# Row E on SyncE's queue, one feature fold for two blocks, and batch 1's folds across spread over steps 24 to 29 on two engines

## The chip, the core and the metric

The kernel runs on one core of a Trainium2 chip. A core has five engines that this document speaks of: PE (TensorE, matrix products, with its weight loads listed apart as PEld), DVE (VectorE), ACT (ScalarE), POOL (GpSimd) and SP (SyncE, which only issues DMAs here). Each engine works through its own list of instructions in order and waits on semaphores for the others. ACT can issue DMAs too; such an issue, and whatever it waits for, stands in ACT's list between its computing instructions. The metric is device time in microseconds (us) of one execution.

## The reference

```python
X = np.fft.fft(x, axis=1); X = np.fft.fft(X, axis=2)     # x: (8, 3008, 256)
t = X.real.astype(np.float32).reshape(24064, 256)
gate = 1.0 / (1.0 + np.exp(-(t @ w_gate)))                # w_gate, w_val: (256, 1536)
out = (gate * (t @ w_val)) @ w_out                        # w_out: (1536, 256)
```

Everything is float32.

## The kernel before, in words

**Tiling.** A batch has S = 3008 rows. A row s, its mirror S-s and the two rows half a batch away are loaded side by side as the four parts `x4[:, 0..3]` of one tile (128 partitions x 4 parts x 6 row groups q x 256 features). Sums and differences of the parts ("folds") shrink the transform over rows, and sums and differences of features d and 256-d shrink the one over features. `fold_ops` lists the folds of a batch: `point` and `first` add the mirrored rows (L405, L409), `across` adds and subtracts parts 0 and 2 (L418), `feat` makes feature sums and differences of one block (L412 to L415). There are two blocks, for even and odd frequencies. The products with cosine and sine tables (`half`, sums into the banks `ev` and `od`) give PK (cosine of the feature sums) and QK (sine of the feature differences), written by `places` (L510, L513) after ACT has copied the bank `ev` (L505). The middle feature, number 128, has its own row: `e_sums` multiplies it with the tables into the bank `pe`, `even`, `rest` and `last` put it together in the tile `er`, and it goes out to the DRAM tensor `ed` (L572) and comes back spread over all partitions as `ek` (`e_rows`, L599).

**Steps.** Then come 288 tokens-by-features steps `i`, twelve to a group of columns (chunk). A step multiplies PK with G1 (`front_a`), ACT copies the result (`part`, L626, tile `ae`), PE adds QK times G2 into the same bank (`front_b`), so `front_b` must wait for `part`. ACT and DVE then gate it (`gate_a`, `gate_b`: L640, L641, L653, L654, L657), POOL forms sums of blocks (`H_SUMS`, L663, tile `sf`), and five steps later `back` multiplies them with output weights (`po`). Order inside a step on DVE: gate_a's L641, gate_b's L653 and L657, copies and sums of a finished chunk (`later`, L747), then the work that `at(i, ...)` put at step i. On ACT: L640, L626, the next step's `seed` (L611, twice), L654.

**The start.** Batch 0 is folded by DVE in three calls of `half_rows`, two row groups each; after each one PE multiplies what is ready: the cosine sums of block 0, row E (`e_`), the cosine sums of block 1. When all three are done come the copies and placements, ACT's first half of the weight job 2 (`weight_parts(2)`: L296, L297), ACT's DMA of row E, ACT's copy of it to `e0` (L837, into the tile `wqk`), the sine sums, ACT's jobs 3 and 5 with the two `ev` copies for QK between and behind them, ACT's DMA of `ek`, and step 0. Steps 0 to 4 take row E by two extra products with `e0`; from step 5 on, `seed` takes it from `ek`. Weight jobs are 512 KB loads by SP in the order 0, 1, then (behind batch 0's rows and tables) 2, 3, 5, 6, 8, 9, 4, 7, each with a pass over ACT (L296, L297), DVE (L306, L307, L309) and POOL (L311), then a product on PE (`ps`) and two ACT copies (L331, L332), and small DMAs of `ge` on SP (L334).

**DMA semaphores.** DMAs from SP and ACT take eight semaphores (DMAHW0 to 7) in turn in program order. An instruction that issues one waits first for the last DMA on its semaphore. In the program's list of waits the DMA of row E waits for DMAHW7, last used by weight job 8, and ACT's `ek` waits for DMAHW2 (job 7) besides row E.

**Batch 1's folds.** Their 24 operations are put at steps given by hand in `slots`: POOL's points and firsts at steps 20 to 24, six `across` on DVE, two each at steps 27, 28 and 29, POOL's feature folds and row sums from 31 on. Batch 1's PK and QK are computed at step 64. Rows E of batches 1 to 7 are made together: sums and the first `places` (in `even`) at step 40, an ACT copy (`rest`) at 41, the second `places` (`last`) and the DMA to `ed` at 42.

Of the kernel before, what the change touches and what calls it, by code (L numbers as in the profile page):

```python
# [12 lines left out]
ALU = mybir.AluOpType  # L13
# [40 lines left out]
NQ = 6  # L54
# [27 lines left out]
def kernel(  # L82
# [10 lines left out]
    nc = tc.nc  # L93
    B, _, _, _, D = xf.shape
    F = moe_w_gate.shape[1]
    P = 128
# [4 lines left out]
    NO = (M // 2) // 2  # L101
# [296 lines left out]
    def fold_ops(b, nq):  # L398
        x4 = X.pop(b)
        if not b:  # L400
            x4 = x4[0:NP]
        ops = []

        def point(e, i, j, q):
            e.tensor_tensor(x4[:, i, q, 1:D], x4[:, i, q, 1:D], x4[:, j, q, D - 1 : 0 : -1],  # L405
                            op=ALU.add)

        def first(e, i, j, q):
            e.tensor_tensor(x4[:, i, q, 0], x4[:, i, q, 0], x4[:, j, q, 0], op=ALU.add)  # L409

        def feat(e, v, r, q):
            e.memset(r[:, q, 0:1], 0.0)  # L412
            e.tensor_tensor(r[:, q, 1:HD], v[:, q, 1:HD], v[:, q, D - 1 : HD : -1],  # L413
                            op=ALU.subtract)
            e.tensor_tensor(v[:, q, 1:HD], v[:, q, 1:HD], v[:, q, D - 1 : HD : -1], op=ALU.add)  # L415

        def across(e, blk, q):
            e.tensor_tensor(x4[:, 1 - blk, q], x4[:, 0, q], x4[:, 2, q],  # L418
                            op=(ALU.add, ALU.subtract)[blk])

        parts = [(x4[:, 1], x4[:, 3]), (x4[:, 0], x4[:, 2])]
        qs = [slice(q, q + nq) for q in range(0, NQ, nq)]
        pool = nc.gpsimd
        if b:

            for i in (0, 2):
                ops += [lambda i=i, q=q: point(pool, i, i + 1, q) for q in qs]
                ops.append(lambda i=i: first(pool, i, i + 1, slice(0, NQ)))
            for blk in range(2):
                ops += [lambda blk=blk, q=q: across(nc.vector if b == 1 else pool, blk, q) for q in qs]  # L430
            ops += [lambda q=q: feat(pool, *parts[1], q) for q in qs]
            for i, op in enumerate((ALU.add, ALU.subtract)):
                for ds in (slice(0, HD), slice(HD, D)):
                    ops.append(lambda i=i, op=op, ds=ds: pool.tensor_tensor(
                        x4[:, 3, i * N3 : (i + 1) * N3, ds], x4[:, 1, 0:N3, ds],
                        x4[:, 1, N3:, ds], op=op))
            parts[0] = x4[:, 3], x4[:, 1]
            slots = x4.rearrange("p i q d -> p (i q) d")

            def turn(q, minus):  # L440

                y = [slots[:, q : q + 16 : 15], slots[:, q + N3 : q + N3 + 10 : 9]]
                if minus:
                    y.reverse()
                nc.vector.scalar_tensor_tensor(
                    out=y[0][:, :, HD:D], in0=y[1][:, :, 0:HD], scalar=(ST[3], ST[4])[minus][:, q : q + 1],
                    in1=y[0][:, :, 0:HD], op0=ALU.mult, op1=ALU.add)
            TURN[b] = [lambda q=q, minus=minus: turn(q, minus) for q in range(N3) for minus in range(2)]
            ops += [lambda q=q: feat(pool, *parts[0], q) for q in qs]
        else:  # L450

            def half_rows(q):
                even, odd = slice(0, 4, 2), slice(1, 4, 2)
                point(nc.vector, even, odd, q)
                first(nc.vector, even, odd, q)
                for blk in range(2):
                    across(nc.vector, blk, q)
                    feat(nc.vector, *parts[blk], q)
            ops += [lambda q=q: half_rows(q) for q in qs]
        for blk, (v, r) in enumerate(parts):  # L460
            if b and blk:
                W[b, blk] = v[:, :, HD:D], r[:, :, HD:D]
                continue
            W[b, blk] = v[:, :, 0:HD], r[:, :, 0:HD], v[:, :, HD : HD + 1]
        return ops
# [40 lines left out]
            return lambda: places(d, blk, sn, a, od)  # L506
        return sums, then, both

    def places(d, blk, sn, ev, od):
        nc.vector.tensor_tensor(d[:, blk : blk + 2 * ev.shape[1] - 1 : 2], ev, od, op=ALU.add)  # L510
        lo, hi = (od, ev) if sn else (ev, od)
        top = M - blk
        nc.vector.tensor_tensor(d[:, top : top - 2 * NO + 1 : -2], lo[:, 0:NO], hi[:, 0:NO],  # L513
                                op=ALU.subtract)

    def whole(b, blk, what):
        _, then, both = seq_group(b, blk, what, (2, 3) if what else (0, 1))
# [8 lines left out]
    def seq_group(b, blk, what, other=None):  # L526
        return half(b, lambda q: W[b, blk][what][:, q, :], PQE[b][what], blk, what == 1, other)
# [14 lines left out]
    def e_sums(m=B - 1):  # L542


        ps = bank("pe", NB - 1)
        at_ = lambda blk, par: slice((2 * blk + par) * TB, (2 * blk + par) * TB + m)

        def sums(*qs):
            for q in qs:
                for blk in range(2):  # L550
                    c0, n = ((0, NE), (NE, NO))[blk]
                    w = x8[:, :, 1 + 2 * blk, q] if m > 1 else W[0, blk][2][:, q]
                    mm(ps[at_(blk, q % 2), 0:n], w, ST[0][0:NP, 0, q, c0 : c0 + n], q < 2, q >= NQ - 2)

        def even():
            er = op.tile([P, NK + 1], F32, name="er", tag="os")[0:m]
            if m == 1:
                E0.append(er)
            nc.vector.memset(er[:, NK:], 0.0)
            a = evp.tile([P, 2 * NJ], F32, name="a", tag="a")[0:m, 0:NE]  # L560
            e1 = evp.tile([P, 2 * NJ], F32, name="a", tag="a")[0:m, 0:NE]
            nc.scalar.copy(a, ps[at_(0, 1), 0:NE])
            nc.scalar.copy(e1[:, 0:NO], ps[at_(1, 0), 0:NO])

            places(er, 0, True, a, ps[at_(0, 0), 0:NE])

            def rest():
                nc.scalar.copy(a[:, 0:NO], ps[at_(1, 1), 0:NO])

            def last():  # L570
                places(er, 1, False, e1[:, 0:NO], a[:, 0:NO])
                (nc.sync if m > 1 else nc.scalar).dma_start(out=ed[1:] if m > 1 else ed[0:1], in_=er)  # L572
            return rest, last
        return sums, even

    def e_joint():
# [17 lines left out]
    def e_rows(i):  # L594

        b, c, _ = groups[i // 3]
        k0, n = chunks[c]
        EK[i // NFT] = ekp.tile([P, CH], F32, name="ek", tag="ek")[:, 0:n]
        (nc.sync if i else nc.scalar).dma_start(out=EK[i // NFT], in_=ed[b : b + 1, k0 : k0 + n].to_broadcast([P, n]))  # L599

    PF, AP, Z = {}, {}, {}
    N1 = 5
# [222 lines left out]
    for i, f in enumerate(fold_ops(0, 2)):  # L825
        q = 2 * i, 2 * i + 1
        f()
        cos[0][0](*q)
        e_(*q)
        cos[1][0](*q)  # L830
    cos[0][1]()()
    cos[1][1]()()
    rest, last_ = e_even()
    rest()
    weight_parts(2)
    last_()
    nc.scalar.copy(e0[0:1], E0[0][:, 0:CH])  # L837
    sin = [seq_group(0, blk, 1, (2 * blk, 2 * blk + 1)) for blk in range(2)]
    for q in range(0, NQ, N3):
        for sums, _, _ in sin:  # L840
            sums(*range(q, q + N3))
# [13 lines left out]
    def at(i, *fs):  # L855
        side.setdefault(i, []).extend(fs)
# [29 lines left out]
    at(3 * i0 + 5, lambda: later_e[0]())  # L886
    at(3 * i0 + 6, lambda: later_e[1]())
    at(3 * i0 + 6, table_again)
    at(4 * i0 - 3, lambda: [at(i, f) for i, f in zip((50, 46, 48, 49, 51, 52), table_odd())])
    for i in range(i0, count, i0):  # L890
        at(i - (8 if i == i0 else 11), lambda i=i: e_rows(i))

    for b in range(B - 1):
        s0 = b * per
        g0 = s0 + 3 * i0 + 4 if b else 5 * i0 + 4


        slots = [i for i in range(s0 - 2 * i0 if b > 1 else s0 if b else 2 * i0, g0 - 2)
                 if i % i0 < (4 if b > 1 else 6)]

        def folds(slots, b=b):
            ops = fold_ops(b + 1, 2)
            for i, f in enumerate(ops):
                at(slots[i * len(slots) // len(ops)], f)
            for i, f in enumerate(TURN.pop(b + 1)):
                at(58 + i if b == 0 else slots[-1] - 1 + i * 4 // 6, f)
        if b == 0:

            slots = [20, 20, 21, 21, 22, 23, 24, 24, 27, 27, 28, 28, 29, 29, 31, 33, 35, 37, 39, 41, 44, 51, 54, 56]
            assert len(slots) == 24  # L910
        at(slots[0] - 1, lambda slots=slots, folds=folds: folds(slots))
        at(g0 - 2, lambda b=b: seq_start(b + 1))
        for blk in (1, 0):
            at(g0, *[lambda b=b, blk=blk, what=what: whole(b + 1, blk, what)() for what in range(2)])
        if b < B - 2:
            at(g0 + 1, lambda b=b: load_x(b + 2))
            for i, f in zip(calm(s0 if b else 3 * i0), mirror_x(b + 2)):
                at(i, f)
# [83 lines left out]
```

## Time and profile before

| | us |
|---|---|
| median of 3 runs (1931.51 to 1933.19) | 1932.86 |
| profiled execution, whole | 1933.04 |
| its span, first to last instruction | 1931.2 |
| PE busy in the span | 1914.2 |
| POOL busy | 1520.4 |
| DVE busy | 1434.4 |
| ACT busy | 1342.4 |

The profile shows one execution. The lines of a timeline give start and duration in us, the engine (a q behind the name marks the issue of a DMA), the source line, operation, output and input tile, and in brackets how long the engine was idle before it and what ended that. Lines of windows give, for a stretch, the busy time of each engine, the granted clock of PE as a share of full speed (PEclk), the busy share of the DMA engines and what they moved. A line "A <- B: total, times, longest" is a wait of A that B ended.

### The profile page before, as it was taken

The page shows a single profiled execution, that of the slowest core. Times are in us where ns is not written, and L with a number is a line of the kernel's source. Part 1 is how long each engine was busy: PE and PEld are TensorE (multiplying, and loading weights), DVE is VectorE, ACT ScalarE, POOL GpSimd, SP SyncE. Part 2 cuts the span into 40 slices and gives each one's busy share as a digit, 9 for nine tenths or more (in the row PEclk, how much of TensorE's full clock was granted, in tenths as well). Part 3 has the DMA queues.
Part 4 walks back from the last instruction along what each step waited for, and adds up shares of the span by engine and source line. Part 5 has one row for each costly group of instructions (what it writes and reads, how often), then busy time and mean ns, then how long its engine had stood idle before and what let it go on. Part 6 is the DMA issues. An engine that isn't in the chain of part 4 may idle for free.

```text
span 1931.2 us, 34216 instructions
## 1 busy us (share of the span) xinstructions
PE 1914.2 (99%) x11164; PEld 1777.5 (92%) x11164; DVE 1434.4 (74%) x3236; ACT 1342.4 (70%) x3148; POOL 1520.4 (79%) x2731
## 2 busy tenths in 40 slices
PE   7999999999999999999999999999999999999999
PEld 5788999999999999999999999999999999999998
DVE  6777887787777777777777777777777777776775
ACT  3776767767777677776777767777677766777775
POOL 2389869988899788987889879888788886877770
PEclk9999999999999999999999999999999999999999
DMA  8352422212021201302122121111200100011001
GB/s 311 86 117 40 106 80 52 55 18 77 15 59 47 79 14 25 79 19 80 21 45 56 18 81 23 47 47 26 82 15 15 24 18 15 15 20 22 15 16 31
DMA packets 172321, 97.02 MB, mean 50 GB/s; under 512 B 134397, under 2 KB 162792, under 8 KB 170096
## 3 DMA queue, kind: packets, MB, share of 16 engines
q1 hardware_dynamic: 171420, 94.19, 20.0%
q8 instruction: 90, 1.47, 0.3%
q14 instruction: 87, 0.71, 0.1%
q10 hardware_dynamic: 692, 0.65, 0.1%
q0 software_dynamic: 32, 0.00, 0.0%
HBM read 70.08 MB, written 46.71 MB: 60 GB/s over the span
## 4 chain that ended last, share of the span: by engine, by line
PE 95%; DMA 2%; POOL 1%; DVE 1%; ACT 1%; SPq 0%; issue 0%; ACTq 0%; POOLq 0%
PE pf L134 49%; PE po L134 41%; PE ev L134 2%; POOL sf L663 1%; PE ps L134 1%; DMA st<-in_stab_dram 1%; DMA raw<-in_moe_w_out_dram 1%; PE od L134 1%; DVE x L418 0%; SPq L191 0%; DVE c L747 0%; DVE z L641 0%; ACT pf L654 0%; ACT ae L626 0%; POOL x L413 0%
## 5 line engine op out<-in xcount | busy, mean ns | idle before, releaser
L663 POOL TENSOR_TENSOR sf<-h 128x168 f32<-128x168 f32 (+1 forms) x920 | 509.5, 572 | 220.9 <-DVE h L657 220.6
L663 POOL TENSOR_TENSOR sf<-h,sf 128x168 f32<-128x168 f32 (+1 forms) x1104 | 616.0, 578 | 59.1 <-DVE h L657 58.7
L134 PE MATMUL pf<-qk,G 128*128 128x252 f32 (+1 forms) x2304 | 583.4, 376 | 6.5 <-ACT ae L626 6.5
L134 PE MATMUL pf<-pk,G 128*128 128x252 f32 (+1 forms) x2304 | 582.9, 376 | 0.0
L611 ACT ACTIVATE pf<-ek,ge 128x252 f32<-128x252 f32 (+1 forms) x1142 | 538.1, 471 | 20.4 <-DMA ge<-G 1.1
L657 DVE TENSOR_TENSOR h<-pf,z 128x252 f32<-128x252 f32 (+1 forms) x576 | 241.6, 419 | 417.4 <-ACT pf L654 417.4
L134 PE MATMUL po<-sf,wf 128*128 128x168 f32 (+1 forms) x2944 | 508.3, 305 | 0.0
L626 ACT ACTIVATE ae<-pf 128x504 f32<-128x504 f32 (+1 forms) x576 | 339.1, 589 | 233.8 <-PE pf L134 231.4
L134 PEld LDWEIGHTS pf<-pk,G 128*128 128x128 f32 x2304 | 436.4, 190 | 53.0 <-issue 2.3
L134 PEld LDWEIGHTS po<-sf,wf 128*128 128x128 f32 x2944 | 453.3, 190 | 8.0
L134 PE MATMUL po<-h,wf 128*128 128x168 f32 (+2 forms) x2584 | 459.7, 306 | 0.0
L134 PEld LDWEIGHTS pf<-qk,G 128*128 128x128 f32 x2304 | 411.4, 190 | 37.5 <-ACT ae L626 8.2
L747 DVE TENSOR_TENSOR c<-c 128x168 f32<-128x168 f32 (+1 forms) x920 | 429.8, 499 | 4.8
L134 PEld LDWEIGHTS po<-h,wf 128*128 128x128 f32 x2584 | 411.5, 190 | 17.0 <-issue 0.9
L641 DVE TENSOR_TENSOR z<-ae,pf 128x504 f32<-128x504 f32 (+1 forms) x576 | 383.7, 666 | 36.4 <-ACT h L640 34.8
L640 ACT ACTIVATE h<-pf 128x252 f32<-128x252 f32 (+1 forms) x576 | 217.6, 378 | 161.8 <-PE pf L134 156.0
L654 ACT ACTIVATE pf<-z 128x252 f32<-128x252 f32 (+1 forms) x576 | 214.0, 372 | 87.6 <-DVE h L653 85.2
L653 DVE TENSOR_TENSOR h<-h,pf 128x252 f32<-128x252 f32 (+1 forms) x576 | 233.0, 404 | 0.0
L663 POOL TENSOR_TENSOR sf<-sf 128x168 f32<-128x168 f32 (+1 forms) x184 | 105.8, 575 | 14.4
L663 POOL TENSOR_TENSOR sf<-sf,h 128x168 f32<-128x168 f32 (+1 forms) x184 | 100.3, 545 | 0.0
L730 ACT COPY c<-po 128x504 f32<-128x504 f32 (+1 forms) x138 | 78.4, 568 | 0.0
L755 DVE STREAM_TRANSPOSE os<-c 128x256 f32<-128x256 f32 x188 | 72.2, 422 | 0.7 <-issue 0.6
(140 smaller groups left out, 905.0 us busy)
## 6 DMA issues: line engine op xcount, KB each, us to landing
x<-xr SPq DMA_DIRECT2D x14, 1536.0 KB
out_dram<-os SPq DMA_DIRECT2D x368, 56.0 KB
xr<-in_xf_dram SPq DMA_DIRECT2D x14, 768.0 KB
xr<-in_xf_dram SPq DMA_DIRECT2D x35, 256.0 KB
ek<-ed SPq DMA_DIRECT2D x39, 126.0 KB
out_dram<-os SPq DMA_DIRECT2D x284, 7.0 KB
x<-in_xf_dram SPq DMA_DIRECT2D x3, 1024.0 KB
st<-in_stab_dram SPq DMA_DIRECT2D x3, 753.0 KB
```

What stands on the lines that cost most here:

```text
L134: nc.tensor.matmul(o, l, r, start=start, stop=stop, skip_group_check=True)
L611: nc.scalar.activation(PF[i][:, g], EK[i // NFT], AF.Copy, scale=ge[:, g, f : f + 1])
L626: nc.scalar.activation(AP[i], PF[i], AF.Copy, scale=2.0)
L640: nc.scalar.activation(H[p][:, fh, 0:n], PF[i][:, 0], AF.Sigmoid)
L641: nc.vector.tensor_tensor(z[:, :, ::-1], AP.pop(i), PF[i], op=ALU.subtract)
L653: nc.vector.tensor_tensor(h[:, fh, 0:n], h[:, fh, 0:n], pf[:, 1], op=ALU.mult)
L654: nc.scalar.activation(pf[:, 0], z[:, 0], AF.Sigmoid)
L657: nc.vector.tensor_tensor(h[:, fh, n:], pf[:, 0], z[:, 1], op=ALU.mult)
L663: nc.gpsimd.tensor_tensor(block(p, dst), block(p, a), block(p, b), op=(ALU.subtract, ALU.add)[op])
L730: (nc.vector.tensor_copy if t == 1 or t == 3 else nc.scalar.copy)(C[0][:, 3 * t * R : 3 * (t + 1) * R], PO[t][:, 0 : 3 * R])
L747: nc.vector.tensor_tensor(t[:, dst * R : (dst + 1) * R], *v, op=(ALU.subtract, ALU.add)[op])
L755: nc.vector.transpose(os_[0][:, s, 0:nb, h, :], t[:, c0 : c0 + nb * TB])
```

## The change

1. Row E of batch 0 goes out on SP's queue, and so does the first `ek`; ACT issues neither.
2. In batch 0's fold the two feature folds of the blocks become one over both (one subtraction and one addition of 128x508 elements in place of two each of 128x254), after both `across`; row E's products stand ahead of the cosine sums in each of the three parts.
3. The sine sums of block 0 take two of the banks that the steps use, those of block 1 the banks 0 and 1 (before: banks 0, 1 and 2, 3).
4. `places` of the last pieces of rows E is split in two; for batches 1 to 7 the second half, and the DMA behind it, move from step 42 to step 43.
5. Batch 1: both `first` stand at step 20, the points go row group by row group, `across` stands for the first two row groups on DVE, one each at steps 24 to 27, and for the third on POOL at steps 27 and 29. Four later POOL operations stand one step earlier (44, 51, 54, 56 become 43, 50, 53, 55).

```diff
-        if b:
+        if b == 1:
+
+            for i in (0, 2):
+                ops.append(lambda i=i: first(pool, i, i + 1, slice(0, NQ)))
+            for q in qs:
+                ops += [lambda i=i, q=q: point(pool, i, i + 1, q) for i in (0, 2)]
+            for q in qs:
+                ops += [lambda blk=blk, q=q, e=pool if q is qs[-1] else nc.vector: across(e, blk, q) for blk in range(2)]
+        elif b:
...
                 for blk in range(2):
                     across(nc.vector, blk, q)
-                    feat(nc.vector, *parts[blk], q)
+                v, r = x4[:, 0:2, q], x4[:, 2:4, q]
+                for to, op in ((r, ALU.subtract), (v, ALU.add)):
+                    nc.vector.tensor_tensor(to[:, :, :, 1:HD], v[:, :, :, 1:HD], v[:, :, :, D - 1 : HD : -1],
+                                            op=op)
+                nc.vector.memset(r[:, :, :, 0:1], 0.0)
...
             def last():
-                places(er, 1, False, e1[:, 0:NO], a[:, 0:NO])
-                (nc.sync if m > 1 else nc.scalar).dma_start(out=ed[1:] if m > 1 else ed[0:1], in_=er)
-            return rest, last
+                places(er, 1, False, e1[:, 0:NO], a[:, 0:NO], (0,))
+
+            def end():
+                places(er, 1, False, e1[:, 0:NO], a[:, 0:NO], (1,))
+                nc.sync.dma_start(out=ed[1:] if m > 1 else ed[0:1], in_=er)
+            return rest, last, end
...
-        (nc.sync if i else nc.scalar).dma_start(out=EK[i // NFT], in_=ed[b : b + 1, k0 : k0 + n].to_broadcast([P, n]))
+        nc.sync.dma_start(out=EK[i // NFT], in_=ed[b : b + 1, k0 : k0 + n].to_broadcast([P, n]))
...
         f()
+        e_(*q)
         cos[0][0](*q)
-        e_(*q)
         cos[1][0](*q)
...
-    sin = [seq_group(0, blk, 1, (2 * blk, 2 * blk + 1)) for blk in range(2)]
+    sin = [seq_group(0, blk, 1, (0, 1) if blk else None) for blk in range(2)]
...
     at(3 * i0 + 6, lambda: later_e[1]())
     at(3 * i0 + 6, table_again)
+    at(3 * i0 + 7, lambda: later_e[2]())
...
-            slots = [20, 20, 21, 21, 22, 23, 24, 24, 27, 27, 28, 28, 29, 29, 31, 33, 35, 37, 39, 41, 44, 51, 54, 56]
+            slots = [20, 20, 20, 21, 21, 22, 23, 24, 24, 25, 26, 27, 27, 29, 31, 33, 35, 37, 39, 41, 43, 50, 53, 55]
```

More of the change, by code (lines that the diff above doesn't have):

```diff
@@ L429, in fold_ops @@
             for blk in range(2):
-                ops += [lambda blk=blk, q=q: across(nc.vector if b == 1 else pool, blk, q) for q in qs]
+                ops += [lambda blk=blk, q=q: across(pool, blk, q) for q in qs]
+        if b:
             ops += [lambda q=q: feat(pool, *parts[1], q) for q in qs]
@@ L507, in half, with places @@
         return sums, then, both
-    def places(d, blk, sn, ev, od):
-        nc.vector.tensor_tensor(d[:, blk : blk + 2 * ev.shape[1] - 1 : 2], ev, od, op=ALU.add)
+    def places(d, blk, sn, ev, od, ends=(0, 1)):
+        if 0 in ends:
+            nc.vector.tensor_tensor(d[:, blk : blk + 2 * ev.shape[1] - 1 : 2], ev, od, op=ALU.add)
         lo, hi = (od, ev) if sn else (ev, od)
         top = M - blk
-        nc.vector.tensor_tensor(d[:, top : top - 2 * NO + 1 : -2], lo[:, 0:NO], hi[:, 0:NO],
-                                op=ALU.subtract)
+        if 1 in ends:
+            nc.vector.tensor_tensor(d[:, top : top - 2 * NO + 1 : -2], lo[:, 0:NO], hi[:, 0:NO],
+                                    op=ALU.subtract)
     def whole(b, blk, what):
@@ L832 @@
     cos[1][1]()()
-    rest, last_ = e_even()
+    rest, *ends = e_even()
     rest()
     weight_parts(2)
-    last_()
+    for f in ends:
+        f()
     nc.scalar.copy(e0[0:1], E0[0][:, 0:CH])
-    sin = [seq_group(0, blk, 1, (2 * blk, 2 * blk + 1)) for blk in range(2)]
+    sin = [seq_group(0, blk, 1, (0, 1) if blk else None) for blk in range(2)]
     for q in range(0, NQ, N3):
```

## The prediction

> **What bounds the kernel now.** I read the page's totals first, then windows, then the waits of PE, and then the timeline at the two places where those waits lie.
>
> ```profile
> span 1931.2 us, 34216 instructions
> PE 1914.2 (99%) x11164; PEld 1777.5 (92%) x11164; DVE 1434.4 (74%) x3236; ACT 1342.4 (70%) x3148; POOL 1520.4 (79%) x2731
> ```
> ```profile
> 20.00:40.00 20.00, 16.10 (x62) 8.65 (x63) 12.31 (x28) 8.23 (x17) 1.29 (x1) 0.98 0.97 356
> 40.00:60.00 20.00, 20.00 (x89) 17.55 (x88) 15.16 (x29) 11.94 (x29) 7.84 (x6) 0.94 0.16 47
> 150.00:200.00 50.00, 46.95 (x278) 41.84 (x278) 39.06 (x82) 33.07 (x78) 43.94 (x82) 1.00 0.18 38
> 200.00:250.00 50.00, 49.70 (x286) 46.50 (x285) 40.97 (x90) 35.71 (x85) 45.43 (x89) 1.00 0.45 103
> ```
> ```profile
> PE pf L134 <- ACT ae L626: 6.5, 5, 3.1
> ```
>
> PE is busy for 1914.2 of 1931.2 us (first number after a window's length), and the change takes no product away. So all that can be won is PE's idle time, 17.0 us, and time at a low clock. 6.5 us of the idle time is one wait, `front_b` on ACT's copy `ae` (L626): 3.1 us once near 39 us, and the rest between 150 and 205 us. The clock is below 1.00 just around the first.
>
> **The first wait (near 39 us).** ACT and DVE rows, then PE, then SP:
>
> ```profile
> 34.18 0.48 ACTq L572 DMA_DIRECT2D ed<-er  x1
> 34.71 0.40 ACT L837 COPY wqk<-er 1x252 f32<-1x252 f32 x1 [3.73 <-DMA wc<-in_moe_w_gate_dram]
> ...
> 37.77 0.45 ACT L505 COPY a<-ev 128x376 f32<-128x376 f32 x1
> 38.36 0.35 ACTq L599 DMA_DIRECT2D ek<-ed  x1
> 38.76 0.59 ACT L626 ACTIVATE ae<-pf 128x504 f32<-128x504 f32 x1 [0.54 <-DMA raw<-in_moe_w_out_dram]
> ```
> ```profile
> 30.32 0.53 DVE L513 TENSOR_TENSOR er<-a 1x376 f32<-1x376 f32 x1
> ...
> 38.72 0.54 DVE L513 TENSOR_TENSOR qk<-od,a 128x376 f32<-128x376 f32 x1
> ```
> ```profile
> 35.16 0.72 PEld L134 LDWEIGHTS pf<-wqk,G 128*128 128x128 f32 x4 [0.54 <-ACT wqk L837]
> 39.40 2.05 PE L134 MATMUL pf<-qk,G 128*128 128x252 f32 x4 [3.12 <-ACT ae L626]
> ```
> ```profile
> 28.85 0.51 SPq L334 DMA_DIRECT2D ge<-G  x1
> 30.26 0.47 SPq L334 DMA_DIRECT2D ge<-G  x1
> ```
>
> Row E is complete at 30.32 + 0.53 = 30.85, but its DMA is issued on ACT at 34.18, when weight job 8 (tile `wc`) has landed. ACT stood still from 34.71 - 3.73 = 30.98; all that ACT does for step 0 is queued behind that issue. With the issue on SP, ACT's copy starts at 30.98, and the work from there to the end of the second `ev` copy, 38.22 - 34.71 = 3.5 us, ends at 34.5. Also the 0.54 us before L626 goes, the issue of `ek` with its wait for job 7. The loads do not hold ACT up again: jobs 3 and 5 free SP's issues at 28.85 and 30.26 (these wait for their semaphores), and ACT wants them at 31.3 and 32.9. QK's last piece moves from 39.26 to about 35.5. So PE decides: it was done with `front_a(0)` at 39.40 - 3.12 = 36.28.
>
> On PE, the weight loads of the products with row E waited 0.54 us for L837 (35.16), which goes; part of that lay beside the products before, so I take 0.3. The merged fold gives another bit:
>
> ```profile
> 15.47 1.21 DVE L405 TENSOR_TENSOR x<-x 128x1020 f32<-128x1020 f32 x1
> ...
> 19.85 1.21 DVE L405 TENSOR_TENSOR x<-x 128x1020 f32<-128x1020 f32 x1
> ...
> 23.88 0.42 DVE L415 TENSOR_TENSOR x<-x 128x254 f32<-128x254 f32 x1
> ```
> ```profile
> 25.78 0.79 PE L134 MATMUL od<-st,x 128*128 128x376 f32 x2
> 26.41 1.43 PE L134 MATMUL ev<-st,x 128*128 128x377 f32 x4
> ```
> ```profile
> L418 DVE TENSOR_TENSOR x<-x x6: 684/690/693, 12.4 to 22.7; 128x512 f32<-128x512 f32 x6
> ```
>
> A third of the fold takes 19.85 - 15.47 = 4.38 us. Four operations of 0.42 become two of 508 elements, 0.69 by the `across` of 512: 4.38 - 1.68 + 1.38 = 4.08. Three thirds win 0.9: the last fold ends at 23.4 instead of 24.3. Row E's products need only `across` and run during the fold, and behind it PE has all four cosine pairs left, 0.63 each (25.78 to 26.41), so the sine sums start at 23.4 + 0.2 for the handover + 2.5 = 26.1 instead of 26.41. That is 0.3. PE ends `front_a(0)` at 36.28 - 0.3 - 0.3 = 35.7; L626 and handovers (38.76 to 39.40, and 0.1 before) take 0.7, so `front_b(0)` starts at 36.4: **3.0 us** earlier. Ends: 2.0, if ACT or QK is a microsecond later than I place it, and 3.3.
>
> **The clock.**
>
> ```profile
> 40.00:41.00 1.00, 1.00 (x4) 0.83 (x3) 0.97 (x3) 1.00 (x3) 0.09 (x1) 0.50 0.75 271
> ```
>
> After that idle time PE ran at half clock. Over the two long windows 20 x 0.02 + 20 x 0.06 = 1.6 us of full clock are missing. PE's gap in front of `front_b(0)` would be 0.7 us; the 1.68 us wait further down kept the clock at 1.00. So I take **1.6 us** off; the ends are 0 (should a gap fall badly) and 1.7. [...]
>
> **The waits from 150 to 205 us.**
>
> ```profile
> 145.08 2.05 DVE L418 TENSOR_TENSOR x<-x 128x512 f32<-128x512 f32 x2
> ...
> 150.30 1.98 DVE L418 TENSOR_TENSOR x<-x 128x512 f32<-128x512 f32 x2
> ...
> 199.31 0.89 DVE L510 TENSOR_TENSOR er<-a 7x376 f32<-7x376 f32 x1
> ```
> ```profile
> 158.32 0.38 ACT L654 ACTIVATE pf<-z 128x252 f32<-128x252 f32 x1 [3.06 <-DVE h L653]
> ```
> ```profile
> 154.44 1.12 PE L134 MATMUL pf<-qk,G 128*128 128x252 f32 x4 [1.24 <-ACT ae L626]
> ...
> 159.53 1.12 PE L134 MATMUL pf<-qk,G 128*128 128x252 f32 x4 [1.68 <-ACT ae L626]
> ...
> 203.16 1.12 PE L134 MATMUL pf<-qk,G 128*128 128x252 f32 x4 [0.29 <-ACT ae L626]
> ```
> ```profile
> 137.90 0.42 DVE L657 TENSOR_TENSOR h<-pf,z 128x252 f32<-128x252 f32 x1 [1.17 <-ACT pf L654]
> ```
>
> In steps 27 to 29 two `across` (about 1.0 each beside POOL, 0.69 without) stand on DVE ahead of the next step's L641 and L653; ACT's L654 waits for L653, and the next `part` stands behind L654. The first pair cost PE nothing, the later two 1.24 and 1.68. Afterwards steps 24 to 26 carry one each, where DVE has 1.17 us to spare, step 27 one beside a copy (half of what was free there before), steps 28 and 29 none: **2.9 us** won. The 0.29 us at 203.16 follows two `er` operations of 0.89 in one step; they are parted, and the **0.3 us** go. What SP issues behind that DMA, table loads apart, comes a step later, and the tables now go ahead of it; SP's stores wait for DVE anyway.
>
> What this costs is POOL's: two `across` more.
>
> ```profile
> 126.06 2.58 POOL L405 TENSOR_TENSOR x<-x 128x510 f32<-128x510 f32 x2
> ...
> 154.14 1.15 POOL L663 TENSOR_TENSOR sf<-h 128x168 f32<-128x168 f32 x2 [0.97 <-DVE h L657]
> ...
> 159.30 1.74 POOL L663 TENSOR_TENSOR sf<-h,sf 128x168 f32<-128x168 f32 x3 [1.53 <-DVE h L657]
> ...
> 178.12 1.54 POOL L663 TENSOR_TENSOR sf<-h,sf 128x168 f32<-128x168 f32 x3
> ...
> 194.91 1.15 POOL L663 TENSOR_TENSOR sf<-h 128x168 f32<-128x168 f32 x2 [2.83 <-DVE h L657]
> ```
> ```profile
> 183.52 0.45 PE L134 MATMUL po<-sf,wf 128*128 128x168 f32 x2
> ```
>
> By the points, 2.58 us for two. POOL has no pause from 159.30 to 192.1 (194.91 - 2.83). Step 36's first two sums end at 178.12 + 1.03 = 179.15, and PE uses them at 183.52: 4.4 us in hand. PE will be 2.9 earlier, POOL 2.58 later, less the 0.97 + 1.53 of waiting for DVE that the late L657 caused: 4.4 - 2.9 - 2.6 + 2.5 = 1.4 us left. I cost it at nothing, with that margin as cover; if it fails, PE waits for `sf` as long as POOL is late. The lower end is the whole 2.9.
>
> **Edits costed at nothing.** The banks of the sine sums: PE shows no wait on a bank there (26.41 follows 25.78 at once), so nothing is to be won; the step banks are read by ACT and DVE before steps 1 and 2 ask for them. `ek` on SP waits behind three loads, until about 39; its first reader is step 5, near 55. Both `first` at step 20 now need both halves of batch 1's load, where the second was first read two steps later; POOL's first read at 126.06 shows no wait, and the load is issued as many us earlier as the steps are. If the half were late, the sums queued behind on POOL would be, too, with some 4 us in hand. The four operations a step earlier fall where POOL has pauses.
>
> **Sum.** 3.0 + 1.6 + 2.9 + 0.3 = 7.8 us, on the profiled 1933.04 (span 1931.2 and 1.8 around it): 1925.2. Against the median 1932.86 it is 1925.0, and I give that.
>
> **Rivals.**
> - *POOL becomes the bound in steps 30 to 40* (chance 0.12). The margin of 1.4 us is a difference of large terms, with POOL full for 30 us. Being 1.4 to 4.3 us later than I count gives back up to the 2.9: 1925.0 + 2.9 = 1927.9. Against it: fewer `across` on DVE should also slow POOL's sums less.
> - *The move to SP saves only the issue* (0.08). ACT would then meet the next late landing, or QK be late, win the issues 0.48 + 0.35 = 0.83, and the idle gap and low clock would stay: 1932.86 - 0.83 - 3.2 = 1928.8. [...] The 3.73 us row speaks against it: what stands on ACT is a wait, and no row of this case yet shows the issue on SP.
> - *Most of it is given back* (0.07): a wait of PE in steps 1 to 12, where weight jobs come about 5 us earlier against loads that do not; 1929 to 1936.
> - *Slower* (0.05). POOL again, from where lateness exceeds 1.4 + 7.8 = 9.2 us at step 36: a seventh more on the 66 us that POOL works from 126 to 192, should every sum stretch beside DVE's spread `across`. At 14 us it gives 1932.86 + 4.8 = 1937.7. Nothing quoted shows such stretching.
>
> **How the numbers follow.** The forecast has 0.68, within 1923.0 to 1926.6 (PE's own 0.3 and 0.1 for the start, a microsecond the other way for ACT). Up to 1929.2 the POOL rival and the issue rival add 0.12 and 0.08; 0.12 is left out above, so the range is 1923.0 to 1929.2, with a little for the runs' own spread. 0.2% is 3.9 us, about what a measurement tells from no change: faster is below 1929.0. The forecast, POOL and most of the issue rival are: 0.87; within 0.2%: 0.08; slower: 0.05.
>
> **What would show it.** Right: `front_b(0)` near 36.4 with a gap under 1 us; clock 1.00 between 36 and 45; no PE wait on `ae` in steps 27 to 43; single L418 rows of about 1.0 us in steps 24 to 27 on DVE and two near 1.3 on POOL; waits of PE below 1 us after 30 us. Wrong: ACT idle before weight job 3 or 5; PE rows with `sf` that wait for POOL; a clock of 0.50 after 20 us.

## The result and the profile after

| | before | after |
|---|---|---|
| median, same chip, six runs each, us | 1931.57 (1931.39 to 1933.19) | 1925.68 (1925.50 to 1925.91) |
| profiled execution, whole | 1933.04 | 1925.74 |
| its span | 1931.2 | 1924.0 |

The ratio is 0.9967, with a 95% interval of 0.9954 to 0.998: the kernel is 0.3% faster. Predicted were 1925.0 us and a range of 1923.0 to 1929.2. Against the profiled execution of before the change is worth 1933.04 - 1925.74 = 7.30 us, where the sum of the prediction had 7.8. One run among all of the experiments, the first of "The queue alone", took 9734.73 us, 5.05 times the median of its set at a recorded mean clock of 1.0, for a reason that no run shows; it is left out of the ranges below. (One number given above is wrong: there are 576 steps, 72 to a batch, not 288.)

The first lines of the page of after, then its windows:

```profile
span 1924.0 us, 34205 instructions
PE 1910.2 (99%) x11164; PEld 1776.2 (92%) x11164; DVE 1430.1 (74%) x3225; ACT 1343.0 (70%) x3148; POOL 1522.6 (79%) x2733
```
```profile
20.00:40.00 20.00, 18.74 (x72) 11.84 (x71) 14.95 (x29) 10.39 (x22) 3.06 (x3) 1.00 1.00 361
40.00:60.00 20.00, 20.00 (x93) 17.32 (x92) 13.70 (x27) 14.02 (x35) 7.41 (x6) 1.00 0.15 42
150.00:200.00 50.00, 48.81 (x293) 44.06 (x291) 38.81 (x81) 33.80 (x80) 47.03 (x88) 1.00 0.40 89
```

PE works 18.74 us of the twenty from 20 to 40 us (before: 16.10), the clock is 1.00 in both first windows (before: 0.98 and 0.94), and from 150 to 200 us PE works 48.81 us (before: 46.95). The waits of PE on the copy `ae` have shrunk from 6.5 to 1.9 us, but one of 1.1 us is new. (L644 of after is L626 of before; L659, L671, L672, L675 and L765 are L641, L653, L654, L657 and L747; L524 and L528 are L510 and L513; L518, L856, L590 and L617 are L505, L837, L572 and L599; L681 and L773 are L663 and L755.)

```profile
PE pf L134 <- ACT ae L644: 1.9, 3, 1.1
```

**The start.** Timeline of after on ACT, SP and PE:

```profile
30.27 0.67 ACT L297 ACTIVATE raw<-raw 128x512 int32<-128x512 uint32 x1
30.84 0.38 ACT L856 COPY wqk<-er 1x252 f32<-1x252 f32 x1
...
33.93 0.47 ACT L518 COPY a<-ev 128x376 f32<-128x376 f32 x1
35.88 0.59 ACT L644 ACTIVATE ae<-pf 128x504 f32<-128x504 f32 x1 [1.48 <-PE pf L134]
```
```profile
33.96 0.32 SPq L590 DMA_DIRECT2D ed<-er  x1
...
38.61 0.41 SPq L617 DMA_DIRECT2D ek<-ed  x1
```
```profile
36.52 1.12 PE L134 MATMUL pf<-qk,G 128*128 128x252 f32 x4 [0.68 <-ACT ae L644]
```

ACT copies row E at 30.84 (before 34.71) and is through at 34.4; it then waits for PE, not PE for it. The wait for the landing of weight job 8 is still there, since row E's DMA leaves at 33.96, only 0.22 us earlier than before: it now stands on SP (0.9 us of SP's waits), and no product waited for what stands behind it there. (In both traces the 961 DMA issues of SP and ACT carry eight semaphore numbers, in turn but for a few at the start and the end; weight job 8 and row E's DMA both carry 118.) `front_b(0)` starts at 36.52 instead of 39.40, with a gap of 0.68 us on PE. Batch 0's fold began 0.18 us later in this execution than in that of before (10.19 against 10.01), so the start as such is worth 2.88 + 0.18 = 3.06 us.

**Steps 27 to 45.** From here on I compare the start of `front_b` in both kernels, step by step; the difference of the two is what has been won up to that step. First rows of before (its rows at 154.44, 159.53 and 203.16 stand in the prediction), then the same six steps of after:

```profile
162.79 1.01 PE L134 MATMUL pf<-qk,G 128*128 128x252 f32 x4
...
199.58 1.01 PE L134 MATMUL pf<-qk,G 128*128 128x252 f32 x4
...
206.41 1.01 PE L134 MATMUL pf<-qk,G 128*128 128x252 f32 x4
```
```profile
148.53 1.01 PE L134 MATMUL pf<-qk,G 128*128 128x252 f32 x4
151.65 1.01 PE L134 MATMUL pf<-qk,G 128*128 128x252 f32 x4
154.78 1.01 PE L134 MATMUL pf<-qk,G 128*128 128x252 f32 x4
...
191.57 1.01 PE L134 MATMUL pf<-qk,G 128*128 128x252 f32 x4
194.70 1.01 PE L134 MATMUL pf<-qk,G 128*128 128x252 f32 x4
199.04 1.12 PE L134 MATMUL pf<-qk,G 128*128 128x252 f32 x4 [1.06 <-ACT ae L644]
```

The lead is 39.40 - 36.52 = 2.88 us at step 0 and 4.38 from step 1 up to the steps with the folds across (the half clock is gone). There it becomes 154.44 - 148.53 = 5.91, then 7.88, then 162.79 - 154.78 = 8.01, and it stays 8.01 to the step at 191.57. Then 203.16 - 194.70 = 8.46, as before's wait of 0.29 us is passed, and 206.41 - 199.04 = 7.37 at the new wait. At the end it is 7.30: after step 45 nothing is won or lost but 0.07.

| term | predicted | measured |
|---|---|---|
| start | 3.0 | 2.88 |
| clock | 1.6 | 4.38 - 2.88 = 1.50 |
| waits at the folds across | 2.9 | 8.01 - 4.38 = 3.63 |
| row E's operations of step 42 | 0.3 | 7.30 - 8.01 = -0.71 |
| sum | 7.8 | 7.30 |

### The profile page after: what moved, and what is told of

It reads as the page before. It is cut to its first block, busy times and chain, and to the rows that moved or that the text cites. A ratio compares the mean times of both kernels' runs of the same rounds, so it can differ in the third digit from the quotient of the medians.

```text
span 1924.0 us, 34205 instructions
## 1 busy us (share of the span) xinstructions
PE 1910.2 (99%) x11164; PEld 1776.2 (92%) x11164; DVE 1430.1 (74%) x3225; ACT 1343.0 (70%) x3148; POOL 1522.6 (79%) x2733
## 4 chain that ended last, share of the span: by engine, by line
PE 97%; DVE 1%; ACT 0%; DMA 0%; issue 0%; SPq 0%
PE pf L134 51%; PE po L134 42%; PE ev L134 3%; PE ps L134 1%; PE od L134 1%; DMA raw<-in_moe_w_val_dram 0%; DVE c L765 0%; DVE x L418 0%; DVE x L469 0%; DVE z L659 0%; ACT ae L644 0%; PE pe L134 0%; ACT pf L672 0%; ACT wl L389 0%; DVE x L409 0%
## 5 line engine op out<-in xcount | busy, mean ns | idle before, releaser
L681 POOL TENSOR_TENSOR sf<-h 128x168 f32<-128x168 f32 (+1 forms) x920 | 510.2, 573 | 218.9 <-DVE h L675 218.6
L681 POOL TENSOR_TENSOR sf<-h,sf 128x168 f32<-128x168 f32 (+1 forms) x1104 | 614.8, 577 | 56.2 <-DVE h L675 55.7
L675 DVE TENSOR_TENSOR h<-pf,z 128x252 f32<-128x252 f32 (+1 forms) x576 | 241.6, 419 | 418.8 <-ACT pf L672 418.8
L644 ACT ACTIVATE ae<-pf 128x504 f32<-128x504 f32 (+1 forms) x576 | 339.2, 589 | 237.7 <-PE pf L134 236.5
L765 DVE TENSOR_TENSOR c<-c 128x168 f32<-128x168 f32 (+1 forms) x920 | 431.0, 501 | 4.8
L659 DVE TENSOR_TENSOR z<-ae,pf 128x504 f32<-128x504 f32 (+1 forms) x576 | 383.7, 666 | 35.3 <-ACT h L658 33.7
L672 ACT ACTIVATE pf<-z 128x252 f32<-128x252 f32 (+1 forms) x576 | 214.0, 372 | 78.1 <-DVE h L671 75.0
L671 DVE TENSOR_TENSOR h<-h,pf 128x252 f32<-128x252 f32 (+1 forms) x576 | 232.9, 404 | 0.0
L681 POOL TENSOR_TENSOR sf<-sf 128x168 f32<-128x168 f32 (+1 forms) x184 | 105.5, 573 | 14.4
L681 POOL TENSOR_TENSOR sf<-sf,h 128x168 f32<-128x168 f32 (+1 forms) x184 | 100.3, 545 | 0.0
L773 DVE STREAM_TRANSPOSE os<-c 128x256 f32<-128x256 f32 x188 | 72.2, 422 | 0.4 <-issue 0.3
```

The source lines that it names most:

```text
L644: nc.scalar.activation(AP[i], PF[i], AF.Copy, scale=2.0)
L659: nc.vector.tensor_tensor(z[:, :, ::-1], AP.pop(i), PF[i], op=ALU.subtract)
L671: nc.vector.tensor_tensor(h[:, fh, 0:n], h[:, fh, 0:n], pf[:, 1], op=ALU.mult)
L672: nc.scalar.activation(pf[:, 0], z[:, 0], AF.Sigmoid)
L675: nc.vector.tensor_tensor(h[:, fh, n:], pf[:, 0], z[:, 1], op=ALU.mult)
L681: nc.gpsimd.tensor_tensor(block(p, dst), block(p, a), block(p, b), op=(ALU.subtract, ALU.add)[op])
```

## The experiments

Three questions: are the three gains those three causes; what is the new wait at step 45; and does POOL have the margin I counted. "Changed kernel" is the one after.

### The queue alone

The kernel before, with the two DMAs moved and nothing else. It was run in two sets.

```diff
-                (nc.sync if m > 1 else nc.scalar).dma_start(out=ed[1:] if m > 1 else ed[0:1], in_=er)
+                nc.sync.dma_start(out=ed[1:] if m > 1 else ed[0:1], in_=er)
...
-        (nc.sync if i else nc.scalar).dma_start(out=EK[i // NFT], in_=ed[b : b + 1, k0 : k0 + n].to_broadcast([P, n]))
+        nc.sync.dma_start(out=EK[i // NFT], in_=ed[b : b + 1, k0 : k0 + n].to_broadcast([P, n]))
```

> The kernel before with one edit: row E of batch 0 and the first ek are issued by SP. My theory: ACT's wait of 3.7 us goes, front_b(0) starts near 36.8 instead of 39.40 with an idle gap of PE under 1 us, so no half clock afterwards; about 1929.0, and all runs close together. Rival (only the issue time is saved): 1930.7, gap of PE over 2 us. The waits near 154 and 160 us stay in both.

> The kernel before with row E's DMA and the first load of ek on SyncE's queue and nothing else, for its profile. Theory (ACT stood behind the DMA's wait): ACT's copy L837 follows DVE's row E within 0.3 us, at about 31 us, front_b(0) starts near 36.9 instead of 39.40 with a gap of PE below 1 us, no half clock near 40 us. Rival (only the issue is saved): ACT stands until 34 us and front_b(0) starts after 38.5.

Measured: 1928.38 us in the first set (1928.32 to 1928.59; ratio 0.9977, interval 0.9968 to 0.9987), 1928.34 in the second. Timeline of ACT and of PE in the second set:

```profile
30.94 0.38 ACT L837 COPY wqk<-er 1x252 f32<-1x252 f32 x1
```
```profile
36.60 1.12 PE L134 MATMUL pf<-qk,G 128*128 128x252 f32 x4 [0.68 <-ACT ae L626]
```

ACT copies row E at 30.94, right behind DVE's last part of it, and PE's gap is 0.68 us. So the two lines alone give 2.80 of the 2.88 us at the start, and 4.5 us against the usual 1932.9 of before: 2.80, the clock's 1.5, and a few tenths at the folds across. The rival by which only the time of issuing is saved (1928.8 in the prediction for the whole change) is refuted: the issues cost 0.48 and 0.35 us, and what was won is five times that. The difference is ACT's computing, which was queued behind what row E's DMA waited for, 3.73 us.

### The slots of batch 1 alone

The kernel before, with part 5 of the change only.

```diff
-            slots = [20, 20, 21, 21, 22, 23, 24, 24, 27, 27, 28, 28, 29, 29, 31, 33, 35, 37, 39, 41, 44, 51, 54, 56]
+            slots = [20, 20, 20, 21, 21, 22, 23, 24, 24, 25, 26, 27, 27, 29, 31, 33, 35, 37, 39, 41, 43, 50, 53, 55]
```

> The kernel before with one edit: batch 1's folds as in the change (firsts, points and across in the new order and places, the third across on POOL). My theory: the PE waits between 150 and 165 us go, front_b rows there come about 3.6 us earlier, 1927.9 in runs without the half clock at the start and 1929.4 in runs with it. Rival (POOL becomes the bound): a gain below 2 us, with PE rows on sf that wait for POOL.

Measured: 1930.79 us (1929.04 to 1931.87, ten runs), ratio 0.9988, interval 0.9978 to 0.9997. The waits at the folds across are gone: from 160 to 198 us `front_b` comes 2.18 us earlier than before, and 1.45 us more of it had been lost at the start, where this execution was longer at half clock, so they are worth 3.6 us here too. But the gain in the end is over a microsecond less than expected. Timeline of PE near 200 us (L635 is L626 of before):

```profile
201.13 1.12 PE L134 MATMUL pf<-qk,G 128*128 128x252 f32 x4 [0.44 <-ACT ae L635]
204.97 1.12 PE L134 MATMUL pf<-qk,G 128*128 128x252 f32 x4 [0.43 <-ACT ae L635]
```

There are longer waits in steps 44 and 45, 0.44 and 0.43 us where before had one of 0.29, though row E's operations are where they were in the kernel before. A loss near step 45 thus comes with the slots, without the split of row E.

### Keeping PE warm without moving anything

The kernel before, with six products that nobody reads between `front_a(0)` and `front_b(0)`, where PE stood idle for 3.12 us.

```diff
+        if i == 0:
+            fill = bank("fill", NB - 1)
+            for _ in range(6):
+                mm(fill[:, 0:WC], dt[:, 0, 0:P], dt[:, 0], True, True)
```

> The kernel before with six products of 128x256 that nobody reads put on PE between front_a(0) and front_b(0), 2.6 us in the 3.1 us gap. My theory (runs of the kernel before differ by 1.5 us because in some of them the gap takes the clock down): all runs near 1931.5, clock 1.00 between 38 and 45 us. Rival (the two levels have another cause): both levels, 1931.5 and 1933.0, stay.

Measured: 1931.38 us (1931.05 to 1931.70, ten runs), the kernel before beside it 1931.44 to 1934.38. Window of the kernel with the filler, and one of the kernel with the slots alone, which shows how bad it can be:

```profile
38.00:48.00 10.00, 9.52 (x45) 8.12 (x44) 9.36 (x15) 6.74 (x16) 3.99 (x3) 1.00 0.48 147
```
```profile
38.44:45.27 6.83, 5.71 (x14) 4.59 (x15) 4.86 (x8) 3.04 (x6) 2.64 (x2) 0.50 0.61 193
```

With the gap filled the clock stays at 1.00, and the runs lie where the lowest runs of the kernel before do; so the half clock after the idle time, and not the idle time itself, makes that kernel's spread.

### Row E unsplit

The changed kernel, both halves at step 42 again.

```diff
+    at(3 * i0 + 6, lambda: later_e[2]())
-    at(3 * i0 + 7, lambda: later_e[2]())
```

> The changed kernel, with both er operations and the DMA at step 42 as before. My theory (the split itself, onto step 43, costs): a wait near 0.3 us as in the kernel before, about 1925.2. Rival (DVE's operations are slower there because POOL is now busy beside them, whatever the split): a wait of 1 us or more stays, 1925.7 or above.

Measured: 1925.72 us (1925.66 to 1925.75), the same as the changed kernel. The time is that of the rival. Two shorter waits take the place of the one of 1.06 us:

```profile
195.14 1.12 PE L134 MATMUL pf<-qk,G 128*128 128x252 f32 x4 [0.44 <-ACT ae L644]
198.99 1.12 PE L134 MATMUL pf<-qk,G 128*128 128x252 f32 x4 [0.43 <-ACT ae L644]
```

The split is worth nothing either way.

### POOL's four late operations back where they were

The changed kernel, with the last four of its slots as before.

```diff
-            slots = [20, 20, 20, 21, 21, 22, 23, 24, 24, 25, 26, 27, 27, 29, 31, 33, 35, 37, 39, 41, 43, 50, 53, 55]
+            slots = [20, 20, 20, 21, 21, 22, 23, 24, 24, 25, 26, 27, 27, 29, 31, 33, 35, 37, 39, 41, 44, 51, 54, 56]
```

> The changed kernel with the last four of POOL's operations of batch 1 put back to steps 44, 51, 54 and 56. Theory (the three chunk sums of step 43 take 2.15 us because POOL works beside them, among others with the 1.09 us operation L443 that was moved to that step): the sums of step 43 fall towards 1.2 to 1.6 us, the wait of PE at step 45 falls from 1.06 to below 0.6, and the time to about 1925.1 to 1925.4. Rival (POOL's own sums there are enough to slow DVE): the sums stay near 2 us, the wait near 1 us, the time within 0.2 of 1925.7.

Measured: 1924.95 us (1924.93 to 1925.06), 0.73 below the changed kernel's 1925.68 of the first set, and the fastest of all; ratio to before 0.9957, interval 0.9945 to 0.997. DVE in step 43 of the changed kernel, POOL beside it, and then the same two of this kernel:

```profile
193.93 2.15 DVE L765 TENSOR_TENSOR c<-c 128x168 f32<-128x168 f32 x3
196.00 0.88 DVE L528 TENSOR_TENSOR er<-a 7x376 f32<-7x376 f32 x1
```
```profile
194.21 1.09 POOL L443 TENSOR_TENSOR x<-x 128x384 f32<-128x384 f32 x1
195.26 1.22 POOL L681 TENSOR_TENSOR sf<-h 128x168 f32<-128x168 f32 x2
```
```profile
193.91 1.69 DVE L765 TENSOR_TENSOR c<-c 128x168 f32<-128x168 f32 x3
195.52 0.53 DVE L528 TENSOR_TENSOR er<-a 7x376 f32<-7x376 f32 x1
```
```profile
194.18 1.22 POOL L681 TENSOR_TENSOR sf<-h 128x168 f32<-128x168 f32 x2
197.91 1.16 POOL L681 TENSOR_TENSOR sf<-h 128x168 f32<-128x168 f32 x2 [2.51 <-DVE h L675]
```

Without the moved POOL operation the three sums take 1.69 us instead of 2.15, and row E's half, which now runs while POOL stands still, 0.53 instead of 0.88: 0.81 us less on DVE in that step. The wait of PE falls from 1.06 to 0.26 us. The lead over the changed kernel is 0.83 us from step 45 to 47 and doesn't grow behind that (0.68 at step 64), past the places of the other three operations, so the gain belongs to the first of the four. The theory held; its sums were a little above what it asked for (1.2 to 1.6), and the time a little below (1925.1 to 1925.4). Slow sums alone cost nothing: beside the same operation, now in step 45, the sums are slow again, as they were there in the kernel before (2.02 us), and no wait of PE follows, since no operation of row E stands near.

```profile
200.38 2.02 DVE L765 TENSOR_TENSOR c<-c 128x168 f32<-128x168 f32 x3
```

### Row E's second half a step later

The changed kernel, second half and DMA at step 44.

```diff
-    at(3 * i0 + 7, lambda: later_e[2]())
+    at(3 * i0 + 8, lambda: later_e[2]())
```

> The changed kernel, with the second half of the er placements and its DMA at step 44 (two chunk sums there) in place of 43 (three). My theory: the new PE wait of 1.06 us near 199 comes from step 43's DVE work (three sums beside POOL and an er operation) and goes: 0.7 to 0.9 us under the changed kernel, about 1924.9. Rival (the wait comes from POOL or PE's own order): no difference, 1925.7.

Measured: 1925.25 us (1925.12 to 1925.27), so 0.43 won instead of 0.7 to 0.9. PE's row of step 45:

```profile
198.22 1.12 PE L134 MATMUL pf<-qk,G 128*128 128x252 f32 x4 [0.34 <-ACT ae L644]
```

A wait of 0.34 us is left: the first half still stands in step 42, ahead of the three slow sums of step 43. With both away from there, in the next experiment, it is gone.

### Both halves later

The changed kernel, the halves at steps 44 and 46.

```diff
-    at(3 * i0 + 6, lambda: later_e[1]())
+    at(3 * i0 + 8, lambda: later_e[1]())
...
-    at(3 * i0 + 7, lambda: later_e[2]())
+    at(3 * i0 + 10, lambda: later_e[2]())
```

> Theory (row E's two operations of 0.88 us cost PE only because they stand in steps where the chunk sums already fill DVE's time; steps 44 and 46 have two sums that take 0.92 to 1.7 us): PE shows no wait on L644 above 0.2 us from step 43 on, about 0.3 to 0.4 us less than with the second half alone at step 44 (1925.25), so 1924.8 to 1925.0 against 1925.7 of the changed kernel. Rival (any place in a chunk's steps costs the same): the wait moves to steps 45 and 47, and the time stays at 1925.2 to 1925.7.

Measured: 1925.45 us (1925.34 to 1925.67). The time lies in the range of the rival, but the waits are not where it had them. The wait at step 45 is gone, and some 1.3 us are won there, but all except 0.2 of it is lost again in the three steps from 207.82 us on. DVE and then PE in those steps:

```profile
204.20 1.46 DVE L528 TENSOR_TENSOR er<-a 7x376 f32<-7x376 f32 x1
...
207.75 0.77 DVE L773 STREAM_TRANSPOSE os<-c 128x256 f32<-128x256 f32 x2 [0.30 <-DMA ed<-er]
```
```profile
207.82 1.12 PE L134 MATMUL pf<-qk,G 128*128 128x252 f32 x4 [0.37 <-ACT ae L644]
211.47 1.12 PE L134 MATMUL pf<-qk,G 128*128 128x252 f32 x4 [0.23 <-ACT ae L644]
```

The second half now takes 1.46 us, beside another operation of POOL (L212, 1.21 us), and DVE's next work, the turning of the finished chunk, waits for the DMA that reads the tile `er`: the turned chunk goes into the same buffers (tag `os` in the kernel).

### Two edits that each won, together

The changed kernel with POOL's four operations back and the second half at step 44 (the two diffs above).

> Two edits that each won something alone, together: the last four of POOL's operations of batch 1 at steps 44, 51, 54 and 56 (1924.95 alone), and the second half of row E's placement at step 44 (1925.25 alone, against 1925.7 of the changed kernel). Theory (both shorten the same wait of PE at step 45): that wait, 0.26 us on PE and about 0.4 in the shift, goes, and the time is 1924.5 to 1924.7, not the 1924.5 minus anything more. Rival (the operation of 0.88 us at step 44 now stands beside the moved POOL operation and makes step 46 late): 1925.0 to 1925.6, with a wait on L644 near 201 or 205 us.

Measured: 1925.99 us (1925.90 to 1926.16), not below either of the two but above both, and above the changed kernel. First PE's row of step 45, then waits of its weight loads:

```profile
197.85 1.12 PE L134 MATMUL pf<-qk,G 128*128 128x252 f32 x4
```
```profile
201.27 0.72 PEld L134 LDWEIGHTS pf<-qk,G 128*128 128x128 f32 x4 [0.26 <-ACT ae L644]
...
205.00 0.72 PEld L134 LDWEIGHTS pf<-qk,G 128*128 128x128 f32 x4 [0.57 <-ACT ae L644]
...
208.38 0.72 PEld L134 LDWEIGHTS pf<-qk,G 128*128 128x128 f32 x4 [0.21 <-ACT ae L644]
```

At step 45 this kernel is 199.04 - 197.85 = 1.19 us ahead of the changed one, and four steps later no longer. Row E's half at step 44 takes 0.88 us beside POOL again, and step 45, into which POOL's operation now falls, has sums of 2.03 us. The rival had the place right (waits near 201 and 205 us) but not the whole size. In step 46 two sums take 1.67 us, against 1.00 with POOL's operations alone put back. DVE and POOL there:

```profile
204.54 1.67 DVE L765 TENSOR_TENSOR c<-c 128x168 f32<-128x168 f32 x2
```
```profile
204.81 1.21 POOL L212 TENSOR_TENSOR st<-st 128x561 f32<-128x561 f32 x1
```

The sums come 0.44 us later than with POOL's operations alone (204.10), and so the whole of POOL's next long operation, 204.81 to 206.02, falls beside them; there it began, at 204.88, when they had 0.22 us left.

### POOL's margin

The changed kernel, with POOL's `across` of step 27 done four times.

```diff
-                ops += [lambda blk=blk, q=q, e=pool if q is qs[-1] else nc.vector: across(e, blk, q) for blk in range(2)]
+                ops += [lambda blk=blk, q=q, e=pool if q is qs[-1] else nc.vector, n=4 if q is qs[-1] and not blk else 1:
+                        [across(e, blk, q) for _ in range(n)] for blk in range(2)]
```

> The changed kernel with three more repetitions of one across on POOL at step 27 (same result, about 4.1 us more for POOL). My theory (POOL has 1.4 to 2.5 us in hand at steps 33 to 39): PE waits for sf, 1.5 to 2.7 us over the changed kernel, 1927.2 to 1928.4. Rival (POOL is far from the path): no difference.

Measured: 1928.29 us (1928.17 to 1928.40). POOL's row, and a wait from the list of PE's weight loads:

```profile
147.73 5.41 POOL L418 TENSOR_TENSOR x<-x 128x512 f32<-128x512 f32 x4
```
```profile
PEld po L134 <- POOL sf L682: 2.0, 2, 1.7
```

Three operations more are 3 x 5.41 / 4 = 4.06 us; the products with `sf` wait 2.0 us for them. Taken as the difference of the two, the margin was 2.0 us, where I had 1.4. The time is 2.61 us above the changed kernel's: those 2.0 us and 0.6 more (1928.29 - 1925.68 - 2.0), lost near step 45.

### The folds and the banks, each undone

The changed kernel with the feature folds block by block and row E's products between the cosine sums:

```diff
-                v, r = x4[:, 0:2, q], x4[:, 2:4, q]
...
+                    feat(nc.vector, *parts[blk], q)
...
-        e_(*q)
         cos[0][0](*q)
+        e_(*q)
```

> The changed kernel with batch 0's feature folds block by block and row E's sums between the cosine sums, as before. My theory: 0.2 to 0.3 us slower, 1925.9 to 1926.0, third fold ends about 0.8 us later. Rival (the merged fold is what lets the sine sums start): 0.8 us or more slower.

And with the old banks of the sine sums:

```diff
-    sin = [seq_group(0, blk, 1, (0, 1) if blk else None) for blk in range(2)]
+    sin = [seq_group(0, blk, 1, (2 * blk, 2 * blk + 1)) for blk in range(2)]
```

> The changed kernel with the sine sums in banks 0, 1 and 2, 3, as before. My theory: no difference within 0.2 us. Rival: with row E out of the way a bank is now late: PE waits on a bank at a weight product ps or at the sine sums, slower by 0.5 us or more.

Measured: 1925.90 us (1925.80 to 1926.14) without the merged folds, so these are worth 0.22. The traces agree: counted from the start of batch 0's fold, the sine sums start at 26.45 - 10.07 = 16.38 us without the merged folds and at 26.39 - 10.19 = 16.20 with them. With the old banks it is 1925.58 (1925.55 to 1925.72), so the new ones are worth nothing.

## Why the prediction was right, and where it was not

**The start: right.** The step "ACT stood behind the DMA's wait, and PE decides once it doesn't" is shown by the queue alone: 2.80 us from two lines. `front_b(0)` came at 36.52, predicted near 36.4. The smaller part, the merged fold at 0.3, was a little too large: undoing it cost 0.22 in the medians. The third part, the weight loads that waited for L837, was taken at 0.3, and some 0.4 us of it came: PE was through with the products ahead of `front_b(0)` at 35.84 instead of 36.28, in an execution that began 0.18 later, which is 0.62 for both parts.

**The clock: right, for the usual run.** 1.50 of the 1.6 us came. The sum stands on the profiled execution of before, 1933.04 us, with a half clock once (3.41 us of it); over 63 runs of it in all, 42 lie from 1932.4 to 1933.6. The six runs of the comparison above had four of the lowest level by chance, hence its ratio of 0.9967; against 1932.9 the gain would be 7.2 us.

**The waits at the folds across: right mechanism, too small.** Priced at 2.9 by PE's idle time of 1.24 + 1.68, they were worth 3.63. The same two rows on PE's weight loads, in the kernel before:

```profile
154.44 0.72 PEld L134 LDWEIGHTS pf<-qk,G 128*128 128x128 f32 x4 [1.50 <-ACT ae L626]
159.53 0.72 PEld L134 LDWEIGHTS pf<-qk,G 128*128 128x128 f32 x4 [1.93 <-ACT ae L626]
```

They wait 1.50 + 1.93 = 3.43 us, and the lead of `front_b` grew by about as much. The step that was mis-sized is thus the reading of a wait from PE's idle time: each of these waits is some 0.25 us longer on the loads, and so is the new one of step 45 (1.31 against 1.06). PE's row doesn't show that part, since the last products ahead end that much later than the last loads: 153.19 against 152.94 us, 157.86 against 157.60, and in after 197.98 against 197.73. DVE took one `across` in a step without a trace on PE, as predicted.

**Row E's operations: the wrong sign.** The step that failed is "they are parted, and the 0.3 us go". The old wait did go, but step 43, into which the second half was moved, became the late one. A second step failed with it, among the edits costed at nothing: "The four operations a step earlier fall where POOL has pauses". One of them, 1.09 us long, fell beside DVE's sums of that very step. Undoing that move (with the three others, at which nothing is won) gives 0.73 us back, the whole of the 0.71 lost after step 42; undoing only the split gives nothing. The sign "waits of PE below 1 us after 30 us" failed here, by 0.06. I had asked whether POOL has time for the operation, and not what it does to DVE, which works on the path. The rows for that were at hand: the `across` on DVE at about 1.0 beside POOL and 0.69 without it.

**POOL: right, by a margin.** No product that reads `sf` waited for it. The margin was 2.0 us instead of 1.4; the rival of POOL as the bound was real, and some two more microseconds on POOL would have brought it.

**The other rivals.** That only the issue is saved, and that the gain is given back in steps 1 to 12, did not come: the lead stays 4.38 us there. Nor did the kernel get slower.

**The sum: in part luck.** It came within 0.5 us of 7.8 because the folds across gave 0.73 more than their term and row E's operations 1.01 less than theirs.

## What to carry to other kernels

Before a DMA is left on a computing engine's queue, look what it waits for and what is queued behind it: the issue took 0.48 us, the wait 3.73. When work is moved to an engine that is off the path, price also what it does to the engine beside it: here an operation of 1.09 us on POOL cost PE 0.73 through slower work on DVE, in a step that was full already; two steps later it costs nothing. And near a step that was already full, two edits that each won did not add up (1924.95 and 1925.25 us alone, 1925.99 together); run such edits together before they are counted.

## What the runs showed of the hardware

**One idle gap, three levels of time.** The 63 runs of the kernel before fall in three groups: 12 at 1931.1 to 1931.8 us, 42 at 1932.4 to 1933.6 and 9 at 1933.8 to 1934.7. The window of the profiled execution of before:

```profile
39.07:42.48 3.41, 3.08 (x7) 2.53 (x8) 3.31 (x6) 2.55 (x5) 1.34 (x1) 0.50 0.74 256
```

At half clock PE was busy for 3.08 us, which costs half of that, 1.54 us (the four products of `front_b(0)` took 2.05 us there and 1.12 in after, at a clock of 1.00), about the distance from one group to the next. The kernel with the slots alone had a stretch of 6.83 us in its profile, twice as long, and that run was the slowest of its ten. The mean clock on record says the same of the 57 runs of before that have it: 1.000 for every run of the first group, 0.999 for every run of the second and 0.998 for every run of the third, and one stretch of 3.41 us at half clock takes 3.41 / 2 / 1931 = 0.0009 off it. So the groups are runs with none, one or two such stretches; the filler, which takes the gap away, leaves only the lowest. In the profiled execution the half clock sets in at 39.07 us, 2.79 us after PE's last product (through at 36.28) and 3.19 us after its last weight load (35.88). Behind the gaps of 1.24 and 1.68 us at the folds across, behind the one of 0.68 us in after, and behind the 5.65 us before PE's first product the clock was 1.00. What it takes for a gap to count, and why some runs of before have no such stretch and some two, no run shows.

**DVE beside POOL.** The same three sums of 128x168 took 2.15 us with POOL's operation of 1.09 among those beside them, 1.69 with POOL's shorter sums alone, and 1.16 in the kernel before, beside POOL's sums from 202.93 us on; row E's half took 0.53 with POOL still, 0.88 beside it and once 1.46. I had expected a fixed surcharge; on row E's half it was 0.35 us beside POOL's sums and 0.93 beside L212.
